# Reordering the start of a joint image and text attention block: scale-weight chunks, batch-1 transposes, shift rows

## The chip, the cores and the metric

The kernel runs on one core of a Trainium2 chip. A core has five engines with instruction streams of their own: TensorE (PE) for matmuls and transposes, VectorE (DVE), ScalarE (ACT), GpSimd (POOL), and SyncE (SP), which here issues transfers. The metric is the device time of one execution in microseconds, and the median of several runs is compared. The span is the time from the first to the last instruction of one profiled execution.

## The reference

Two batches of 256 image tokens and 32 text tokens, width D = 1152, bfloat16. Each stream is normalized, modulated, projected to Q, K and V, attended jointly, projected back, gated and added to its input.

```
mod_i = (silu(c) @ wmod_img).reshape(B, 6, 1, D)      # shift, scale, gate are the first three; text alike
hi    = layernorm(x_img) * (1 + sci) + shi            # text: ht, with its own weights
qi, ki, vi = split(hi @ wqkv_img)                     # text: qt, kt, vt
q, k, v = concat(text, image) along the tokens
p   = softmax(q @ k^T * D**-0.5)
a   = p @ v
out_i = x_img + gai * (a[image] @ wo_img)             # text alike
```

## The kernel before

The width is cut into KT = 9 column tiles of 128; the 512 image rows are four row tiles (0 and 1 are batch 0, 2 and 3 batch 1). Every weight matrix is a tile of 128 x 9 x 1152 in one of five slots, and is loaded by SP's queue in the order of the code (lines 96 to 116): x_img in two transfers, the scale part of the modulation weights (`w_sc_i`) in chunks of weight rows given by `SCC` (line 99), the V weights (`w_v_i`) in chunks of 1, 2, 3 and 3 rows, then the shift weights, Q, K and the rest whole.

The image V is not made from the modulated input. The kernel keeps two transposed inputs: `hS_i`, normalized x times (1 + scale), for V (the shift's part of V is worked out apart, in `shift_v_rows`, and added when attention is evicted), and `xT_i`, modulated in place with scale and shift, for Q and K.

The start runs as follows, in the order written out by hand. Nearly every PE instruction passes `mm` or `tr` (lines 61 and 64), which pin it in program order, as `pin` does for the DVE and ACT operations of this stage.

- `warm_up(n)` issues n matmuls of 512 columns on zeros, whose result nobody reads.
- `x_transposes(k0, b)` (line 204) does six PE transposes of three column tiles of one batch into one PSUM tile, and returns a function that issues the copy to `xT_i` (line 214). The PSUM tile is from the pool `ps_tr` (two banks) for the first two of batch 0, else from `ps_mm` (six banks).
- `sc_cols(r0, r1)` (line 198) adds the weight rows r0 to r1 to the scale sums, nine matmuls of 2 columns a row, into one `ps_mm` bank. When row 8 is in, DVE adds 1 (line 273), and `x_scale(k0, k1, b)` makes `hS_i`, one DVE operation for each column tile.
- `v_open(ids, k0, k1)` (line 227) does the V matmuls (512 columns each) of the tiles `ids` for the weight rows k0 to k1. A tile (i, cc) is row tile i and column half cc, and holds one `ps_mm` bank from its first matmul until it is evicted after row 8. `A0` is four tiles of batch 0, `A1` two of batch 1: six banks in all. Tiles (2, 1) and (3, 1) and the last 128 columns (`v_last`) follow later.
- `mod_rows_of(w_sh_i, sT32)` does the 36 matmuls of the image shift. DVE transposes the result (line 302), and DVE and ACT modulate `xT_i` (lines 314 and 317). The x_txt transfer stands behind that on ACT's queue (line 318).

A bank of a pool is taken again when the readers of its last content are done, so a matmul or a transpose into it can wait on ACT or DVE.

Of the kernel before, what the change touches and what calls it, by code (L numbers as in the profile page):

```python
# [14 lines left out]
def kernel(  # L15
# [14 lines left out]
    nc = tc.nc  # L30
# [4 lines left out]
    B, NI, D = x_img.shape  # L35
    NT = x_txt.shape[1]
    P = 128
    KT = D // P
# [19 lines left out]
    pin = tc.keep_in_program_order  # L58

    def mm(*a, **k):  # L60
        return pin(nc.tensor.matmul(*a, **k))  # L61

    def tr(*a, **k):
        return pin(nc.tensor.transpose(*a, **k))  # L64
# [17 lines left out]
    K8 = KT - 1  # L82
# [13 lines left out]
    for b in range(B):  # L96
        nc.sync.dma_start(x_i[:, b * TPB:(b + 1) * TPB, :], x_img[b].rearrange("(p t) d -> p t d", t=TPB))  # L97

    SCC = (0, 3, 5, 7, K8, KT)
    for r0, r1 in zip(SCC, SCC[1:]):  # L100
        nc.sync.dma_start(w_sc_i[:, r0:r1, :], sc_v[:, r0:r1, :])  # L101
    for r0, r1 in ((0, 1), (1, 3), (3, 6), (6, KT)):
# [23 lines left out]
    def warm_up(n):  # L126
        for _ in range(n):
            mm(wps[:], lhsT=warm[:, 0:P], rhs=warm[:], start=True, stop=True)
# [24 lines left out]
    def evac(out_ap, in_ap):  # L153
        if evac_idx[0] % 2 == 0:
            nc.vector.tensor_copy(out_ap, in_ap)  # L155
        else:
            nc.scalar.copy(out_ap, in_ap)  # L157
        evac_idx[0] += 1
# [27 lines left out]
    def ln_norm(x_ap, mean, rstd, np_, out_ap):  # L186
        pin(nc.vector.tensor_scalar(out_ap, x_ap, mean, rstd[0:np_, :], op0=ALU.subtract, op1=ALU.mult))
# [10 lines left out]
    def sc_cols(r0, r1):  # L198
        for kt in range(r0, r1):
            for j in range(KT):  # L200
                mm(sc_ps[:, j, :], lhsT=w_sc_i[:, kt, j * P:(j + 1) * P], rhs=sT[:, kt, :],
                   start=(kt == 0 and j == 0), stop=(kt == KT - 1), skip_group_check=True)

    def x_transposes(k0, b):
        tr_pool = b == 0 and k0 < 6
        tp = (ps_tr if tr_pool else ps_mm).tile([P, 3, NI], bf, tag="tr" if tr_pool else "mm", name="tp")
        for kt in range(k0, k0 + 3):
            for t in range(TPB):
                i = b * TPB + t
                tr(tp[:, kt - k0, t * P:(t + 1) * P], xn_i[:, i, kt * P:(kt + 1) * P], ident[:])  # L210
        dst = xT_i[:, k0:k0 + 3, b * NI:(b + 1) * NI]

        def copy_out():
            pin(nc.scalar.copy(dst, tp[:]) if b == 0 or k0 == 6 else nc.vector.tensor_copy(dst, tp[:]))

        return copy_out

    def x_scale(k0, k1, b):
        for kt in range(k0, k1):
            pin(nc.vector.tensor_scalar(hS_i[:, kt, b * NI:(b + 1) * NI], xT_i[:, kt, b * NI:(b + 1) * NI],  # L220
                                        sc1_i[:, kt, b:b + 1], None, op0=ALU.mult))
# [5 lines left out]
    def v_open(ids, k0, k1, kt_major=True):  # L227
        for key in ids:
            if key not in accs:
                accs[key] = ps_mm.tile([P, VW], f32, tag="mm", name="vps")  # L230
        loop = [(kt, key) for kt in range(k0, k1) for key in ids] if kt_major else \
            [(kt, key) for key in ids for kt in range(k0, k1)]
        for kt, (i, cc) in loop:
            mm(accs[(i, cc)][:], lhsT=hS_i[:, kt, i * P:(i + 1) * P], rhs=w_v_i[:, kt, cc * VW:(cc + 1) * VW],
               start=(kt == 0), stop=(kt == KT - 1), skip_group_check=True)
            if kt == KT - 1:
                evac(v_i[:, i, cc * VW:(cc + 1) * VW], accs[(i, cc)][:])

    A0 = [(0, 0), (1, 0), (0, 1), (1, 1)]
# [16 lines left out]
    r3, r2 = ln_rstd(m3[:, 1:2], P), ln_rstd(s2[:, 2:3], P, sign=-1.0)  # L256
    ln_norm(x_i[:, 3, :], m3[:, 0:1], r3, P, xn_i[:, 3, :])
    ln_norm(x_i[:, 2, :], s2[:, 0:1], r2, P, xn_i[:, 2, :])
    x_transposes(0, 0)()
    x_transposes(3, 0)()  # L260
    x_transposes(6, 0)()
    sc_cols(0, 3)
    warm_up(3)
    sc_cols(3, 5)
    warm_up(1)
    sc_cols(5, 7)
    x_transposes(0, 1)()
    out31 = x_transposes(3, 1)
    sc_cols(7, K8)
    sc_cols(K8, KT)  # L270
    out61 = x_transposes(6, 1)
    out61()
    pin(nc.vector.tensor_scalar_add(sc1_i[:], sc_ps[:], 1.0))
    x_scale(0, 3, 0)
    x_scale(0, 3, 1)
    out31()
    for b in range(B):
        x_scale(3, 6, b)
    for b in range(B):
        x_scale(6, KT, b)  # L280
    v_open(A0, 0, 3)
    v_open(A1, 0, 3)
    v_open(A0 + A1, 3, KT - 2)
    v_open(A0 + A1, KT - 2, KT, kt_major=False)
# [4 lines left out]
    def group(w, kt, g):  # L289
        return w[:, kt, :].rearrange("p (c g l) -> p g c l", g=NGG, l=LW)[:, g]  # L290

    def mod_rows_of(w, lhs):
        gps = ps_tr.tile([P, KT, LW], f32, tag="tr")
        for kt in range(KT):
            for g in range(NGG):
                mm(gps[LW * g:LW * g + LW], lhsT=lhs[:, kt, :], rhs=group(w, kt, g),
                   start=(kt == 0), stop=(kt == KT - 1), tile_position=(0, LW * g))
        return gps

    def mod_cols_of(gps, name):  # L300
        t = const.tile([P, KT, LW], f32, name=name)
        nc.vector.transpose(t[:].rearrange("p c l -> p (c l)"), gps[:].rearrange("p c l -> p (c l)"))
        return t

    p_sh = mod_rows_of(w_sh_i, sT32)
    sh_i = mod_cols_of(p_sh, "shc")
    v_open([(2, 1)], 0, 4)
    nc.vector.tensor_copy(shT32[:, :, 0:B], sh_i[:, :, 0:B])
    hT_i = xT_i
    for kt in range(KT):  # L310
# [5 lines left out]
            else:  # L316
                nc.scalar.activation(h, h, ACT.Identity, bias=sh_i[:, kt, b:b + 1], scale=sc1_i[:, kt, b:b + 1])
    pin(nc.scalar.dma_start(x_t[:], xt_flat[:, :]))
    v_open([(2, 1)], 4, KT)
    v_open([(3, 1)], 0, KT)  # L320

    def v_last():
# [301 lines left out]
```

## Time and profile before

| | |
|---|---|
| median of 13 runs | 122.09 us (121.58 to 123.31) |
| the profiled execution: its time, its span | 121.76 us, 120.0 us |
| PE busy | 114.0 us, 95% of the span |
| VectorE, ScalarE, GpSimd busy | 56.0, 34.4, 11.1 us |
| moved by DMA | 40.88 MB, 341 GB/s over the span |
| V matmuls (128x512) | 325 ns mean of one with the last ones' 128 columns, 18.0 us |

In the 40 slices each digit is the busy share of 3 us in tenths. A row of a timeline gives the start and the busy time in us, engine, line, operation, tiles and count, and in brackets how long the engine stood before it and what ended that. [...] Line 61 is the helper `mm` and line 64 the helper `tr`. A row of the chain is start, duration and what it was; a row of the waits gives the total in us, how often, and the longest. SPq and ACTq are transfers being issued on these queues, and the time to landing runs from the issue.

### The profile page before, as it was taken

Reading aid. Unit: us, or ns where it says so; the run is one execution under the profiler, and the core shown is the slowest. Engines: PE = TensorE matmul, PEld = TensorE weight load, DVE = VectorE, ACT = ScalarE, POOL = GpSimd, SP = SyncE. Lnnn points to the kernel's source line nnn. Section 1 sums busy time; section 2 is a strip of 40 time slices with the busy share of each in tenths; the row PEclk is TensorE's granted clock in tenths of the full one; section 3 lists DMA queues with packets and bytes.
Section 4 is the critical chain, followed back from the end, with each engine's and each line's share of the span. In section 5 each row is a group of like instructions: output and inputs, shape, how many; then the busy total and the mean of one; then the engine's idle time right before and its main releaser. Section 6 shows DMA issues by size and latency. Waiting matters only on the chain.

```text
span 120.0 us, 2599 instructions
## 1 busy us (share of the span) xinstructions
PE 114.0 (95%) x1112; PEld 67.3 (56%) x1121; DVE 56.0 (47%) x146; ACT 34.4 (29%) x73; POOL 11.1 (9%) x28
## 2 busy tenths in 40 slices
PE   5999889999999999999999999999999999999970
PEld 2248734445664444544448448486777766567650
DVE  1677590066837222131721203037785756666670
ACT  4899600046713104201011111125348610000000
POOL 7400000000000000000000000000222707100000
PEclk9999999999999999999999999999999999999998
DMA  4999999999999999999999999999999992420232
GB/s 134 368 376 390 401 403 413 412 413 413 404 374 413 404 411 413 413 410 414 404 413 409 418 399 414 410 408 409 415 398 409 416 367 66 148 98 0 98 81 72
DMA packets 18502, 40.88 MB, mean 341 GB/s; under 512 B 907, under 2 KB 1435, under 8 KB 18491
## 3 DMA queue, kind: packets, MB, share of 16 engines
q1 hardware_dynamic: 17616, 39.56, 84.6%
q0 software_dynamic: 480, 0.89, 2.3%
q10 hardware_dynamic: 395, 0.26, 0.7%
q8 instruction: 9, 0.15, 0.5%
q14 instruction: 2, 0.02, 0.0%
HBM read 39.38 MB, written 1.34 MB: 339 GB/s over the span
## 4 chain that ended last, share of the span: by engine, by line
PE 83%; DMA 9%; SPq 3%; DVE 1%; issue 1%
PE ps L61 51%; PE vps L61 14%; DMA t<-in_wqkv_img_dram 9%; PE gps L61 6%; PE aps L61 6%; PE sps L61 4%; SPq L101 2%; PE pT_ps L64 1%; SPq L97 1%; DVE tmp L565 1%; DVE o L566 0%; SPq L103 0%; PE tpt L64 0%
## 5 line engine op out<-in xcount | busy, mean ns | idle before, releaser
L61 PE MATMUL ps<-xT_i,t 128*128 128x512 bf16 x156 | 35.5, 379 | 0.4 <-issue 0.2
L61 PEld LDWEIGHTS <-t 128*128 128x128 bf16 x405 | 22.8, 98 | 19.4 <-issue 0.7
L61 PE MATMUL ps<-t,aT 128*128 128x384 bf16 (+3 forms) x153 | 20.2, 308 | 0.0
L61 PE MATMUL vps<-t,hS_i 128*128 128x512 bf16 (+1 forms) x106 | 18.0, 325 | 0.7 <-DVE hS_i L220 0.3
L61 PEld LDWEIGHTS <-aT 128*128 128x128 bf16 (+1 forms) x153 | 13.0, 101 | 7.1 <-issue 0.5
L61 PEld LDWEIGHTS <-hS_i 128*128 128x128 bf16 x108 | 9.0, 98 | 9.4 <-issue 0.8
L155 DVE CAST qkT<-ps 128x512 bf16<-128x512 f32 (+1 forms) x6 | 3.8, 635 | 15.4 <-PE ps L61 15.4
L61 PE MATMUL wps<-warm 128*128 128x512 bf16 x26 | 8.8, 494 | 1.3 <-DVE warm L121 1.2
L435 POOL DMA_DIRECT2D mod_scratch<-g_sb x4 | 2.5, 633 | 80.0 <-ACT g_sb L157 80.0
L565 DVE TENSOR_TENSOR tmp<-ps,gb 128x384 bf16<-128x384 f32 (+2 forms) x13 | 6.8, 526 | 6.4 <-PE ps L61 6.3
L333 DVE TENSOR_SCALAR qkT<-ps 128x512 bf16<-128x512 f32 (+1 forms) x5 | 3.3, 665 | 10.8 <-PE ps L61 10.8
L335 ACT ACTIVATE qkT<-ps 128x512 bf16<-128x512 f32 (+1 forms) x6 | 3.3, 552 | 15.5 <-PE ps L61 15.5
L157 ACT CAST qkT<-ps 128x512 bf16<-128x512 f32 (+1 forms) x5 | 2.8, 564 | 16.6 <-PE ps L61 16.6
L155 DVE CAST v_i<-vps 128x512 bf16<-128x512 f32 x5 | 3.4, 688 | 8.3 <-PE vps L61 8.3
L61 PE MATMUL aps<-pT,v_i 128*128 128x288 bf16 x36 | 6.7, 287 | 0.0
L61 PE MATMUL gps<-t,sT 128*32 128x288 bf16 x180 | 6.4, 287 | 0.0
L61 PEld LDWEIGHTS <-warm 128*128 128x128 bf16 x27 | 2.9, 117 | 5.2 <-issue 2.8
L537 DVE TENSOR_SCALAR aT<-aps,svc 128x288 bf16<-128x288 f32 x9 | 4.7, 518 | 2.4 <-PE aps L61 2.3
L61 PEld LDWEIGHTS <-sT 128*32 128x32 bf16 x180 | 4.3, 96 | 2.1 <-issue 1.5
L157 ACT CAST v_i<-vps 128x512 bf16<-128x512 f32 x4 | 2.3, 585 | 11.0 <-PE vps L61 11.0
L61 PE MATMUL sps<-qkT 128*128 128x288 bf16 (+1 forms) x54 | 5.5, 287 | 0.0
L539 ACT ACTIVATE aT<-aps,svc 128x288 bf16<-128x288 f32 x9 | 4.5, 500 | 2.5 <-PE aps L61 2.5
(94 smaller groups left out, 105.2 us busy)
## 6 DMA issues: line engine op xcount, KB each, us to landing
t<-in_wmod_txt_dram SPq DMA_DIRECT2D x3, 2592.0 KB, 18.9
t<-in_wqkv_txt_dram SPq DMA_DIRECT2D x3, 2592.0 KB, 15.7
t<-in_wmod_img_dram SPq DMA_DIRECT2D x2, 2592.0 KB, 18.6
t<-in_wqkv_img_dram SPq DMA_DIRECT2D x2, 2592.0 KB, 22.5
t<-in_wo_img_dram SPq DMA_DIRECT2D x1, 2592.0 KB, 18.0
t<-in_wo_txt_dram SPq DMA_DIRECT2D x1, 2592.0 KB
t<-in_wqkv_img_dram SPq DMA_DIRECT2D x2, 864.0 KB, 11.7
x_i<-in_x_img_dram SPq DMA_DIRECT2D x2, 576.0 KB, 4.1
```

The source lines that it names most:

```text
L61: return pin(nc.tensor.matmul(*a, **k))
L64: return pin(nc.tensor.transpose(*a, **k))
L97: nc.sync.dma_start(x_i[:, b * TPB:(b + 1) * TPB, :], x_img[b].rearrange("(p t) d -> p t d", t=TPB))
L101: nc.sync.dma_start(w_sc_i[:, r0:r1, :], sc_v[:, r0:r1, :])
L155: nc.vector.tensor_copy(out_ap, in_ap)
L157: nc.scalar.copy(out_ap, in_ap)
L333: nc.vector.tensor_scalar_mul(out_ap, in_ap, SCALE)
L335: nc.scalar.mul(out_ap, in_ap, SCALE)
L435: nc.gpsimd.dma_start(gsc[si, b, :].rearrange("(g j) -> g j", g=NGG), g_sb[b:P:32, :])
L537: nc.vector.tensor_scalar(dst, aps[:], bias, None, op0=ALU.add)
L539: nc.scalar.activation(dst, aps[:], ACT.Identity, bias=bias)
L565: nc.vector.tensor_mul(tmp[:, 0:n], ps[:, 0:n], gb[:, b, c0:c0 + n])
```

## The change

The first scale chunks are rows 0 to 3 and 4 to 6 instead of 0 to 2, 3 to 4 and 5 to 6, and three of the four warm-up matmuls between them are gone. The copies of columns 3 to 5 go to DVE and the others to ACT, in both batches. Batch 1's three groups of transposes move: the first stays behind scale row 6, the second moves behind row 8, and the third to behind the first three weight rows of `A0`; the scalings follow in a new order. The shift rows move from before V tile (2, 1) to behind it, and this tile is no longer cut in two.

```diff
-    SCC = (0, 3, 5, 7, K8, KT)
+    SCC = (0, 4, 7, K8, KT)
...
-            pin(nc.scalar.copy(dst, tp[:]) if b == 0 or k0 == 6 else nc.vector.tensor_copy(dst, tp[:]))
+            pin(nc.vector.tensor_copy(dst, tp[:]) if k0 == 3 else nc.scalar.copy(dst, tp[:]))
...
-    x_transposes(0, 0)()
-    x_transposes(3, 0)()
-    x_transposes(6, 0)()
-    sc_cols(0, 3)
-    warm_up(3)
-    sc_cols(3, 5)
+    for out in [x_transposes(k0, 0) for k0 in (0, 3, 6)]:
+        out()
+    sc_cols(0, 4)
     warm_up(1)
-    sc_cols(5, 7)
-    x_transposes(0, 1)()
-    out31 = x_transposes(3, 1)
+    sc_cols(4, 7)
+    out01 = x_transposes(0, 1)
     sc_cols(7, K8)
     sc_cols(K8, KT)
-    out61 = x_transposes(6, 1)
-    out61()
+    out31 = x_transposes(3, 1)
+    out01()
     pin(nc.vector.tensor_scalar_add(sc1_i[:], sc_ps[:], 1.0))
     x_scale(0, 3, 0)
-    x_scale(0, 3, 1)
+    v_open(A0, 0, 3)
+    out61 = x_transposes(6, 1)
     out31()
-    for b in range(B):
-        x_scale(3, 6, b)
-    for b in range(B):
-        x_scale(6, KT, b)
-    v_open(A0, 0, 3)
+    out61()
+    for k0 in (0, 3, 6):
+        for b in range(B):
+            if k0 or b:
+                x_scale(k0, k0 + 3, b)
     v_open(A1, 0, 3)
     v_open(A0 + A1, 3, KT - 2)
     v_open(A0 + A1, KT - 2, KT, kt_major=False)
...
+    v_open([(2, 1)], 0, KT)
     p_sh = mod_rows_of(w_sh_i, sT32)
     sh_i = mod_cols_of(p_sh, "shc")
-    v_open([(2, 1)], 0, 4)
...
     pin(nc.scalar.dma_start(x_t[:], xt_flat[:, :]))
-    v_open([(2, 1)], 4, KT)
     v_open([(3, 1)], 0, KT)
```

## The prediction

> **What bounds the kernel now.** I read the 40 slices first, then the chain that ended last, then the waits of PE (TensorE), then the timelines of PE, ScalarE (ACT) and VectorE (DVE) around the start of the V matmuls.
>
> ```profile
> PE   5999889999999999999999999999999999999970
> DMA  4999999999999999999999999999999992420232
> ```
>
> PE and the DMA engines are both full, so the slices don't say which sets the end. The chain (start, duration, what) does:
>
> ```profile
> 4.92 10.84 DMA t<-in_wqkv_img_dram
> 15.76 0.04 issue
> 15.80 0.38 PE vps L61
> 16.18 0.05 issue
> 16.23 10.52 PE vps L61 x48
> 26.76 1.22 PE gps L61 x36
> ```
>
> The second chunk of the V weights (rows 1 and 2) lands at 15.76. From 15.80 the chain is PE work, piece after piece, up to 115.88; only two DVE operations on the last output follow. So the end is set by when the V matmuls get their second weight chunk, plus every PE instruction and every PE wait behind that moment. The waits of PE in the first 45 us (total us, times, longest) agree:
>
> ```profile
> PE vps L61 <- DVE hS_i L220: 0.3, 1, 0.3
> PE vps L61 <- DMA t<-in_wqkv_img_dram: 0.3, 1, 0.3
> ```
>
> Ahead of 15.80 PE has slack; behind it there is none. The rows at the seam (start, busy us, idle before in brackets):
>
> ```profile
> 13.18 0.67 PE L61 MATMUL sc_ps<-sT,t 128*128 128x2 bf16 x18
> 13.71 0.49 PE L64 MATMUL tp<-ident,xn_i 128*128 128x128 bf16 x6
> 14.51 1.04 PE L61 MATMUL vps<-t,hS_i 128*128 128x512 bf16 x4 [0.31 <-DVE hS_i L220]
> 15.80 10.95 PE L61 MATMUL vps<-t,hS_i 128*128 128x512 bf16 x49 [0.26 <-DMA t<-in_wqkv_img_dram]
> ```
>
> The six transposes at 13.71 are the last of batch 1 (columns 6 to 8). PE then waits for DVE, does the four V matmuls that need weight row 0, and waits for the landing. The copy of those six:
>
> ```profile
> 14.24 0.80 ACT L214 COPY xT_i<-tp 128x768 bf16<-128x768 bf16 x1 [1.11 <-PE tp L64]
> ```
>
> This copy, too, is over before 15.80: it costs nothing today.
>
> **Part 1: first chunks and warm-ups, 0.** The first scale chunk grows from 3 rows to 4. The 3-row chunk lands at 9.13 (issued 1.63, 7.5 to landing), the next 2 rows at 10.6 (2.10 + 8.5): 0.73 us a row, so 4 rows land at about 9.87. PE is at its scale matmuls at 9.95 today; nothing is lost. The chunk up to row 6 ends with the same byte as before, at about 12.0, which is when PE waits 0.2 us for it today. Behind that come 27 small matmuls in place of 18 (18 took 0.47 from start to next start: 27 take 0.70, to 12.74), six transposes in place of twelve (0.67 for 12: 0.33, to 13.08), row 7 (0.24), and row 8, which lands at 13.44 (3.94 + 9.5). So the scale sums end at about 13.7, as today (13.71). The three dropped warm-up matmuls lie in the wait for the 12.0 landing and give nothing back.
>
> One transfer less shifts the rest of SP's queue: in the built program a transfer waits for the one eight places ahead. The fourth V chunk now waits for the second x_img transfer (landed about 5.7) instead of the first scale chunk, and is issued there instead of at 9.12. All bytes keep their order in a queue that moves 389 to 415 GB/s in every 3 us between 9 and 33 us, so landings don't move: 0. Bounds: 0.1 us later; 0.4 us earlier, since PE's four row-0 matmuls end their slots at 14.51 + 4 x 0.219 = 15.39 and it can't use the landing before.
>
> [...] The row first: eight warm-ups from 1.23 took 3.59 us (0.45 each) and V matmuls from 16.23 took 10.52/48 = 0.219 each, so a half-rate PE is plain in the spacing here (the granted clock reads 1.00 for both). Between the last early warm-up (8.73) and 14.51 PE has four wide matmuls today and will have one, with 81 two-column matmuls and short gaps of up to about 0.7 us. [...]
>
> **Part 2: order of transposes, +1.18 us.** Copies change engine (batch 0 columns 3 to 5 to DVE, 0.55; batch 1 columns 0 to 2 to ACT, 0.80): both land before the scale sums are used at 13.88, or are needed only after 15.8. Batch 1's columns 3 to 5 transposes move to the place of the old last six (13.7), ahead of V, in slack. The first V matmul still waits for DVE's first scaling (sum + 1 at 13.88, scaling from 14.17), so 14.51 stands, and the four row-0 matmuls are done before 15.76.
>
> But the last six transposes now stand behind all twelve matmuls of the first four V tiles, so behind the landing. Eight matmuls from 15.80 bring PE to T = 15.80 + 8 x 0.219 = 17.55. There:
>
> - The six transposes take PE 0.33 (half of 12 in 0.67), up to T + 0.33. Before, they filled slack; here nothing covers them.
> - Then V tile (2,0), row 0, goes at once: it takes the bank of the columns 3 to 5 transposes, copied by DVE at about 15.3.
> - Then V tile (3,0), row 0, needs a bank. The pool has six: four hold the open V tiles (0,0), (1,0), (0,1), (1,1), one has just gone to (2,0), and the sixth holds those transposes. In the built program this matmul waits on ACT, which can only be their copy. By the rows above the last transpose result is there 0.49 after the first started, ACT starts 0.04 later, and copies for 0.80: T + 1.33. About 0.07 passes from the end of an engine's write to PE's start (DVE's first scaling, 14.17 + 0.27, to PE at 14.51): T + 1.40.
>
> Without the edit (3,0) would start at T + 0.22. PE is 1.18 us late: 0.33 for transposes and 0.85 standing. Everything of V, shift rows and Q is queued behind that matmul. Bounds: 0.33, if the bank were free, to 1.5, if the copy starts 0.3 later.
>
> DVE loses nothing: its eighteen scalings end at 18.25 today; now the last three wait for that copy (18.88) and end about 19.6, while PE wants them at weight row 6, about 23.9. Weight rows 3 to 5 have landed by 18.1 and 6 to 8 by 20.2, ahead of PE today and more so then.
>
> **Part 3: shift rows one V set later, 0.** The 36 shift matmuls go behind the nine of V tile (2,1) instead of before them: the same PE work in another order. Today they start without a wait, at 26.69, on weights that landed just before (issued 10.59, and to landing):
>
> ```profile
> t<-in_wmod_img_dram SPq DMA_DIRECT2D x1, 2592.0 KB, 16.0
> ```
>
> 10.59 + 16.0 = 26.6: this execution has no wait there to remove. With the move they end at about 27.98 + 1.18 + 1.97 = 31.13 (1.97 is nine matmuls). Behind them hang DVE's transpose and twelve modulations, which end 3.9 us after the rows today (31.86 against 27.98): 35.0. Q starts at 35.19 + 1.18 = 36.4, so 1.3 us of cover stands; without it each late us would cost one. The x_txt transfer, queued on ACT behind the modulations, goes from 28.56 to about 31.7 and lands (6.4) at 38.1 in place of 35.0; its statistics on DVE, 36.08 today and else 37.3, start 0.8 later. The Q eviction queued behind them on DVE is late by under 1 us with five more banks rotating, and the text transposes, 46.95 today, have 7 us of slack. The Q weights land at 33.7 (12.01 + 21.7). SP's later weight loads that wait for PE move with PE; GpSimd's queue is not touched.
>
> **Sum.** 0 + 1.18 + 0. Span 120.0 to 121.2; the profiled time 121.76 to 122.94. The median of the runs is 0.33 above the profiled execution, so I predict **123.2** for the median (+0.9%). From no change, a measurement here can tell about 0.5%, 0.61 us.
>
> **Rivals.**
> 1. *The stall isn't there, only the transposes cost.* +0.33: 122.4. For it: a pool that hands out banks in another order. Against it: six banks, five held, and the wait on ACT in the built program. Chance 0.06.
> 2. *The shift weights are late in the usual run (not slower).* In this execution they land 0.1 us before use. Where DMA is a little slower, today's kernel stands at 26.7 and the changed one, which comes 3 us later, doesn't. The price is that wait, minus 1.18: from 0.57 us of wait on the change is within 0.5%, at 1.18 it is even (122.1), and only beyond 1.8 is it faster. For it: the 0.1 us margin, and runs up to 123.31. Against it: the median is only 0.33 above a run with no such wait, and a slow DMA delays 15.76 in both kernels. Chance 0.12.
> 3. [...] Chance 0.07.
> 4. *My mechanism*: 0.75, with 0.8 to 1.5 us, so 122.9 to 123.6.
>
> **How the numbers follow.** Below 122.4 lie most of rival 2 and half of rival 1; above 123.9 rival 3 and a little of mine: 122.4 to 123.9 leaves out about 2 in 10. Faster: the far end of rival 2 and an earlier second chunk with it, 0.04. Same: the rest of rival 2 and most of rival 1, 0.13. Slower: 0.83.
>
> **What would show it.** In the changed profile: scale sums ending at about 13.7; the V wait for the second chunk still ending near 15.8; six transposes at about 17.5; a PE wait of about 0.8 us on ACT's copy (line 214) ahead of V tile (3,0); shift rows ending near 31; the chain pure PE from there, and a span of about 121.2. The prediction is wrong if the second chunk lands far from 15.8, if PE doesn't stand at the copy, if the V matmuls are spaced over 0.3 us, or if the runs of before turn out to stand at the shift rows.

## The result and the profile after

The changed kernel takes 124.14 us in the median of 11 runs (123.56 to 125.68), the kernel before 122.21 us over the 48 runs beside it: ratio 1.017, 95% interval 1.0136 to 1.0203. It is slower by 1.9 us where I forecast 1.1, and outside the range of 122.4 to 123.9. The ratios in this document leave out the longest executions of a kernel, and below these are mostly ones in which PE's clock fell, so medians and counts by granted clock stand beside them.

The first row that differs is the granted clock over the 40 slices, before:

```profile
PEclk9999999999999999999999999999999999999998
```

And after, with the row of the DMA engines:

```profile
PEclk9999869999999999999999999999999999999999
DMA  4999999999999999999999999999999942301222
```

Slices 5 and 6 (12 to 18 us) fall. In stretches of 0.2 us the clock is 1.00 up to 14.3, 0.50 to 17.7, and 1.00 again: one fall of 3.4 us, and V starts inside it. The 3.41 us ahead of it and the fall itself (stretch, its length, PE busy, count, clock, DMA share, GB/s):

```profile
10.91:14.32 3.41, 2.21 (x68) 1.00 1.04 402
14.32:17.73 3.41, 2.92 (x9) 0.50 1.04 406
```

PE's timeline (start, busy us, idle before) at the seam:

```profile
12.27 0.83 PE L61 MATMUL sc_ps<-sT,t 128*128 128x2 bf16 x27 [1.11 <-DMA t<-in_wmod_img_dram]
12.96 0.49 PE L64 MATMUL tp<-ident,xn_i 128*128 128x128 bf16 x6
13.29 0.84 PE L61 MATMUL sc_ps<-sT,t 128*128 128x2 bf16 x18
13.99 0.53 PE L64 MATMUL tp<-ident,xn_i 128*128 128x128 bf16 x6
14.79 2.31 PE L61 MATMUL vps<-t,hS_i 128*128 128x512 bf16 x5 [0.28 <-DVE hS_i L220]
17.32 1.67 PE L61 MATMUL vps<-t,hS_i 128*128 128x512 bf16 x6 [0.22 <-issue]
18.83 0.50 PE L64 MATMUL tp<-ident,xn_i 128*128 128x128 bf16 x6
19.16 0.38 PE L61 MATMUL vps<-t,hS_i 128*128 128x512 bf16 x1
20.21 10.95 PE L61 MATMUL vps<-t,hS_i 128*128 128x512 bf16 x49 [0.67 <-ACT xT_i L214]
```

A few matmuls are missing from the traces. Here it is the one warm-up left in this stretch (only its weight load is on record, at 11.00), so that the wait of 1.11 is nearer 0.9, and one of the first twelve V matmuls, which is the 0.22 at 17.32.

The V matmuls from 14.79 are 0.43 us apart until about 17.7, against 0.219 in the kernel before (10.52/48). There one lasts 0.38 by the profile, so they overlap, and what one costs is read from the distance of the starts. At 20.21 PE has waited for ACT's copy, as forecast. The chain of the changed kernel shows the same two pieces in a row:

```profile
14.79 2.31 PE vps L61 x5
...
17.32 1.67 PE vps L61 x6
18.99 0.35 PE tp L64 x6
19.34 0.02 issue
19.36 0.81 ACT xT_i L214
20.17 0.04 issue
20.21 7.93 PE vps L61 x36
```

Further down the chain leaves PE for the softmax of DVE and ACT, which it never did before, and comes back at the first attention matmul. The wait of PE there:

```profile
PE aps L61 <- DVE pT L519: 0.3, 1, 0.3
```

The profiled executions (121.76 and 124.25 us, spans 120.0 and 122.3) can be set side by side step by step:

| | before | after | late by |
|---|---|---|---|
| first V matmul | 14.51 | 14.79 | 0.28 |
| first twelve V matmuls of `A0` end (18.83 is the start of the next transposes; 15.80 + 8 x 0.219 before) | 17.55 | 18.83 | 1.28 |
| first matmul of V tile (3,0) (17.55 + 0.22 before) | 17.77 | 20.21 | 2.44 |
| first Q matmul | 35.12 | 37.59 | 2.47 |
| first attention matmul | 88.97 | 91.76 | 2.79 |
| last PE piece of the chain ends | 115.88 | 118.67 | 2.79 |

The last scale chunk landed at 13.71 instead of 13.44, which is 0.27 of the 0.28. The twelve V matmuls took 4.04 us, where full clock makes it 12 x 0.219 = 2.63: 1.41 for the clock. Before, the same twelve took 3.04 with 0.41 of waiting for the second V chunk, and this wait is gone. Transposes and copy add 1.16, the attention 0.32. After the chain's last PE piece the changed kernel needs about 0.4 less to the end of its span, which leaves about 2.3, the difference of the spans.

In all 12 executions whose clock is recorded the mean granted clock of the changed kernel is 0.986 or 0.972: one stretch of 3.4 us at half clock in 122 us, or two. Seven executions with one took 123.87 in the median, five with two 125.23.

### The profile page after: what moved, and what is told of

It is laid out like the page before. It is cut to its first block, busy times and chain, and to the rows that moved or that the text cites. A ratio compares the mean times of both kernels' runs of the same rounds, so it can differ in the third digit from the quotient of the medians.

```text
span 122.3 us, 2591 instructions
## 1 busy us (share of the span) xinstructions
PE 113.7 (93%) x1108; PEld 67.0 (55%) x1118; DVE 56.0 (46%) x146; ACT 34.5 (28%) x73; POOL 11.1 (9%) x28
## 4 chain that ended last, share of the span: by engine, by line
PE 77%; DMA 8%; DVE 6%; ACT 2%; SPq 2%; issue 1%; DVEq 0%; ACTq 0%
PE ps L61 50%; PE vps L61 15%; DMA t<-in_wmod_img_dram 8%; PE aps L61 6%; PE gps L61 4%; ACT e L473 2%; SPq L101 1%; DVE nmx L470 1%; DVE pb L477 1%; DVE pb L479 1%; ACT xT_i L214 1%; SPq L97 1%; PE sps L61 1%; DVE rs L475 1%; DVE tmp L561 1%
## 5 line engine op out<-in xcount | busy, mean ns | idle before, releaser
L61 PE MATMUL vps<-t,hS_i 128*128 128x512 bf16 (+1 forms) x105 | 19.3, 338 | 1.3 <-ACT xT_i L214 0.7
L61 PE MATMUL wps<-warm 128*128 128x512 bf16 x23 | 6.7, 452 | 1.2 <-DVE warm L121 1.2
L61 PE MATMUL aps<-pT,v_t 128*128 128x288 bf16 x18 | 5.1, 286 | 0.0
L61 PE MATMUL ps<-hT_t,t 128*128 128x64 bf16 x162 | 5.1, 193 | 0.0
```

## The experiments

Theory A: the late transposes cost 1.18 us as forecast, and the dropped warm-ups let the clock fall. Theory B: the clock falls because of the coarser chunk or the new order. "Fell" counts executions with a mean granted clock of 0.99 or less; "clock up" is the median of the others, beside that of the kernel before in the same runs.

| kernel | median | ratio (95%) | fell | clock up, kernel before |
|---|---|---|---|---|
| changed | 124.14 | 1.017 (1.0136 to 1.0203) | 12 of 12 | none |
| changed, warm-ups back | 122.63 | 1.004 (1.001 to 1.006) | 1 of 12 | 122.63, 122.20 |
| before, without three warm-ups | 123.92 | 1.003 (0.999 to 1.007) | 10 of 12 | 122.25, 122.20 |
| before, last transposes late | 123.71 | 1.013 (1.010 to 1.016) | 3 of 7 | 123.48, 122.20 |
| changed, warm-ups back, other bank | 121.83 | 0.995 (0.992 to 0.998) | 2 of 11 | 121.39, 122.20 |
| before, chunks 4, 3, 1, 1 | 121.63 | 0.997 (0.994 to 1.000) | 2 of 12 | 121.53, 121.97 |
| before, shift rows later | 122.57 | 1.002 (0.997 to 1.006) | 5 of 12 | 121.86, 121.97 |
| before, six tiles on row 0 | 122.94 | 1.008 (1.005 to 1.011) | 6 of 7 | 122.48 (one), 121.97 |
| changed, warm-ups back, transposes early | 121.98 | 0.999 (0.996 to 1.001) | 5 of 12 | 121.80, 121.97 |
| changed, two warm-ups | 124.26 | 1.012 (1.008 to 1.016) | 5 of 6 | 122.94 (one), 121.94 |
| other bank, six warm-ups | 123.12 | 1.007 (1.003 to 1.010) | 8 of 12 | 122.12, 121.94 |
| before, chunks, shift rows, six warm-ups | 121.60 | 0.998 (0.995 to 1.001) | 3 of 12 | 121.46, 121.94 |
| changed, warm-ups back but earlier | 123.88 | 1.012 (1.008 to 1.015) | 10 of 12 | 122.84 (two), 122.03 |
| other bank, six warm-ups, again | 122.36 | 1.001 (0.997 to 1.005) | 4 of 9 | 122.07, 122.03 |

The kernel before itself fell in 16 of the 104 executions that ran beside these.

**The warm-ups put back in the changed kernel.**

```diff
     sc_cols(0, 4)
-    warm_up(1)
+    warm_up(4)
     sc_cols(4, 7)
```

> The changed kernel with the three dropped warm-up matmuls put back (four in a row behind scale row 3). Theory A (the late transposes cost 1.18 us, and the dropped warm-ups let PE's clock fall for one or two windows of 3.4 us): the granted clock is that of the kernel before (0.997), the V matmuls are 0.22 us apart from the first on, PE still stands about 0.7 us at ACT's copy, and the time is 1.2 us over the kernel before (ratio 1.010). Theory B (the clock falls because of the coarser chunk or the new order, whatever the warm-ups): granted clock stays at 0.986, ratio stays at 1.016.

The clock stays up in 11 of 12, and 1.5 us of the median are gone (124.14 - 122.63; the kernel before had the same median beside both, 122.21 and 122.24). Its timeline has the V matmuls at full pace and the same wait for ACT's copy:

```profile
11.04 0.81 PE L61 MATMUL wps<-warm 128*128 128x512 bf16 x3
12.05 0.83 PE L61 MATMUL sc_ps<-sT,t 128*128 128x2 bf16 x27 [0.20 <-DMA t<-in_wmod_img_dram]
...
14.70 2.97 PE L61 MATMUL vps<-t,hS_i 128*128 128x512 bf16 x11 [0.31 <-DVE hS_i L220]
17.51 0.50 PE L64 MATMUL tp<-ident,xn_i 128*128 128x128 bf16 x6
17.84 0.38 PE L61 MATMUL vps<-t,hS_i 128*128 128x512 bf16 x1
18.89 10.95 PE L61 MATMUL vps<-t,hS_i 128*128 128x512 bf16 x49 [0.67 <-ACT xT_i L214]
```

From the first late transpose to V tile (3,0) it is 18.89 - 17.51 = 1.38 us, and 1.40 was forecast. Theory B falls as the cause of the 12 in 12. But what is left over the kernel before is 0.4 us and not 1.2; some part of the change must win back.

**The warm-ups alone taken from the kernel before.**

```diff
     sc_cols(0, 3)
-    warm_up(3)
     sc_cols(3, 5)
```

> The kernel before without its three warm-up matmuls behind scale row 2; nothing else. Theory A: the clock falls to half for 3.4 us as the V matmuls start; at 0.43 us apart from 14.5 to 17.65 PE does about 7 of them where it did 12, so about 1.1 us is lost (ratio 1.009), and about 2.5 us where the clock falls for two windows. Theory B: no fall, ratio 1.000.

The clock fell in 10 of 12, and the median is 1.7 us up; the two others took 122.25, no more than the kernel before with its clock up. So the warm-ups' time costs nothing and their absence costs the clock. The profiled execution is one of the two, so no trace shows where the clock falls in this kernel.

**The late transposes alone.**

```diff
-    out61 = x_transposes(6, 1)
-    out61()
...
     v_open(A0, 0, 3)
+    out61 = x_transposes(6, 1)
+    out61()
```

(In this kernel the scalings of columns 6 to 8 follow the copy.)

> The kernel before with one thing moved: the last six transposes of batch 1 and their copy stand behind the first three weight rows of the first four V tiles. Theory A: granted clock as before, 0.33 us of transposes behind the landing of the second V chunk and about 0.8 us of standing at ACT's copy: 1.2 us (ratio 1.010). Rival (the stall is a follower of the slow clock, or the bank is free): 0.35 us at most (ratio 1.003).

With the clock up (four executions) 123.48 against 122.20: 1.28 us, the forecast of transposes and stall to 0.1. It fell in 3 of 7, with all warm-ups in place, which theory A doesn't say.

**The bank.** The warm-ups back, and:

```diff
-        tr_pool = b == 0 and k0 < 6
+        tr_pool = k0 < 6 if b == 0 else k0 == 6
```

> The changed kernel with the warm-ups put back and the last six transposes of batch 1 in a bank of the two-bank pool, so that V tile (3,0) needn't wait for their copy. Theory A: the clock stays up and the stall is gone; what is left is 0.33 us of transposes behind the landing (ratio 1.003). Rival (PE stands there for another reason than the bank, such as the scalings on DVE): still about 1.2 us (ratio 1.010).

PE's wait for ACT's copy is gone from the waits, and V tile (3,0) follows the transposes at once:

```profile
16.50 0.50 PE L64 MATMUL tp<-ident,xn_i 128*128 128x128 bf16 x6
16.84 11.17 PE L61 MATMUL vps<-t,hS_i 128*128 128x512 bf16 x50
```

So it was the bank. With the clock up this kernel is 1.24 us below the one with the warm-ups back only; 0.83 of it is the wait (18.89 against 17.84 + 0.22), and nothing here accounts for the rest. That it beats the kernel before here (0.995) did not hold when a close relative ran on another chip (below).

**The chunks alone.** What wins back? In the traces of the two kernels with the old chunks in this set PE stands longer than 0.26 us for the second V chunk: 1.35 us without the warm-ups, 0.89 with the late transposes (the profile names DVE, whose scalings were done over 1 us before). The wait without the warm-ups is the longest of the first row's two, the other is in the second row:

```profile
PE vps L61 <- DVE hS_i L220: 1.7, 2, 1.4
17.26 0.58 PE L61 MATMUL vps<-t,hS_i 128*128 128x512 bf16 x1 [0.89 <-DVE hS_i L220]
```

In the two with the new chunks the fifth V matmul, the first to need that chunk, starts only 0.2 us later than its slot.

```diff
-    SCC = (0, 3, 5, 7, K8, KT)
+    SCC = (0, 4, 7, K8, KT)
...
-    sc_cols(0, 3)
-    warm_up(3)
-    sc_cols(3, 5)
-    warm_up(1)
-    sc_cols(5, 7)
+    sc_cols(0, 4)
+    warm_up(4)
+    sc_cols(4, 7)
```

> The kernel before with the first scale chunks as in the changed kernel (4, 3, 1, 1 rows) and all four warm-up matmuls behind the first. The changed kernel with its warm-ups back came out cheaper than its stall of 0.85 us and 0.33 us of transposes, because V weight rows 1 and 2 were there when PE wanted them. Theory C (one transfer less lets the second V chunk land earlier): PE doesn't wait for it after the four row-0 matmuls, ratio 0.994. Theory F (where the 16 KB fetch of instructions on one DMA engine falls sets when that chunk lands: at the start of V in the kernel before, about 1 us later where twelve PE instructions fewer stand ahead of V): the count of PE instructions ahead of V is unchanged here, the fetch still falls at the start of V, PE still waits 0.3 us or more for the chunk, ratio 1.000.

0.44 us faster with the clock up, ratio 0.997, its interval just under 1. The 54 V matmuls of the first six tiles run on with hardly a wait (the row doesn't break at the fifth, which is 0.1 us late):

```profile
14.96 11.93 PE L61 MATMUL vps<-t,hS_i 128*128 128x512 bf16 x54 [0.31 <-DVE hS_i L220]
```

Theory C got over half of its gain. Theory F falls as I wrote it: the fetch came between 15.75 and 16.0, about 1 us behind the start of V, with as many PE instructions ahead as before. Over all traces the two still go together. In the five with the old chunks the fetch starts 0.9 to 2.7 us before the second V chunk lands (at 15.7 to 17.2). In those with the new chunks and the clock up it starts no more than 0.2 us before the first matmul on that chunk, which comes 0.1 to 0.3 us late. No run separates the fetch from the number of transfers.

**The shift rows alone.**

```diff
+    v_open([(2, 1)], 0, KT)
     p_sh = mod_rows_of(w_sh_i, sT32)
     sh_i = mod_cols_of(p_sh, "shc")
-    v_open([(2, 1)], 0, 4)
...
-    v_open([(2, 1)], 4, KT)
     v_open([(3, 1)], 0, KT)
```

> The kernel before with the shift rows behind V tile (2,1), nothing else. My step: no wait stands at the shift rows, so 0 (ratio 1.000). Rival 2 of the prediction (the shift weights are late in usual runs): 0.3 us or more faster (ratio 0.997 or less).

Ratio 1.002 (0.997 to 1.006), with the clock up 0.11 us less: no change that can be told. In this trace, with the old chunks, the fifth V matmul starts at 15.77, 0.29 us late, against 0.41 in the kernel before and 1.5 without the warm-ups, so the wait changes from execution to execution. The clock fell in 5 of 12, against 4 of 30 of the kernel before beside it, although this edit lies 12 us behind the start of V. Where it fell isn't on record, but counts of this size say little about an edit; 12 of 12 against 1 of 12 does.

**Six tiles on row 0**, to cover that wait (with the shift rows as above):

```diff
-    v_open(A0, 0, 3)
-    v_open(A1, 0, 3)
-    v_open(A0 + A1, 3, KT - 2)
+    v_open(A0 + A1, 0, KT - 2)
```

(The copies of batch 1's columns 0 to 2 and 3 to 5 go to ACT and DVE, the second ahead of the scalings.)

> The kernel before with six V tiles instead of four on weight row 0, so that PE has 0.44 us more of work before it needs the second V chunk; the copy of batch 1's columns 3 to 5 comes earlier to free the bank, and the shift rows stand behind V tile (2,1). If PE's wait for that chunk is what starts the PE-only chain, the wait shrinks by up to 0.44 us: ratio 0.9965. If the chain starts elsewhere (DVE's scalings): 1.000.

It fell in 6 of 7, and the one other took 122.48. The expectation missed. In its trace, which fell, PE does the first 63 V matmuls without a wait for that chunk, but the first ones at half clock, so whether the wait is covered at full clock can't be read from it.

**The transposes early again**, in the changed kernel with its warm-ups:

```diff
     out31 = x_transposes(3, 1)
     out01()
+    out61 = x_transposes(6, 1)
...
-    v_open(A0, 0, 3)
-    out61 = x_transposes(6, 1)
     out31()
     out61()
+    v_open(A0, 0, 3)
```

> The changed kernel with the warm-ups back and the last six transposes ahead of V again: its chunks and its place of the shift rows, without stall and without transposes behind the landing. Theory C: 1.18 us less than the changed kernel with warm-ups back alone (ratio 1.004), so ratio 0.994. Theory F: the fetch falls at the start of V again, the wait for the second V chunk is back, ratio 1.000.

0.17 us under the kernel before with the clock up, between the two theories. Chunks and shift rows alone make -0.44 - 0.11 = -0.55. The rest is the wait at attention: every trace of the changed kernel and of those built from it shows 0.3 to 0.4 us there, and none of those built from the kernel before does. In the changed kernel the third of the five softmax exponentials on ACT starts only when DVE has scaled the second tile's weights, a wait that the kernel before doesn't have:

```profile
  DVE nmx L470: 2.5, 3
  DVE pb L479: 1.3, 1
```

(What ACT waited for around the tile `e` in the changed kernel: total us, times.) -0.55 + 0.33 = -0.22 agrees with -0.17. In its own trace, where V starts at 13.60, the first V matmuls on the second and third V chunk are also late, by 0.3 and 0.4. The source there is the same in both; why an edit at 10 to 35 us makes the built program wait differently at 86 us I haven't tried.

**How many warm-ups.**

```diff
-    warm_up(1)
+    warm_up(2)
```

> The changed kernel with two warm-up matmuls behind scale row 3, where it has one, the kernel before four. In the traces so far the clock fell where the 3.4 us ahead of the fall held no or one matmul of 512 columns (the changed kernel, the late transposes alone, six tiles on row 0) and stayed where they held three or more (warm-ups put back, the early transposes). If that count decides, two lie at the edge: between a tenth and nine tenths of the executions fall, and the median lies between 122.6 and 124.1. If it is only the gap in PE's work (about 0.9 us here, 1.1 with one), nearly all fall as with one, and the median is 124.0.

It fell in 5 of 6; the median of the six is 124.26. And this trace breaks my count: its clock falls at 15.57, and the 3.4 us ahead hold three V matmuls.

```profile
12.15:15.57 3.42, 2.76 (x60) 1.00 1.04 404
15.57:18.98 3.41, 3.41 (x9) 0.50 1.04 405
```

**Two more, ahead of V.** As the other bank, and:

```diff
+    warm_up(2)
     v_open(A0, 0, 3)
```

> The changed kernel with its warm-ups back, the last six transposes in the two-bank pool, and two more warm-up matmuls where PE waits for DVE's first scaling ahead of V. They fill 0.3 us of standing and should cost 0.0 to 0.1 us; if matmuls in the window decide, the clock falls in fewer executions than without them (2 of 11), and the ratio is 0.992 to 0.994, the best so far. If the filled wait delays V, 0.997.

A clear miss: fell in 8 of 12, 123.12. **The parts that gained, together**: the kernel before with the chunks, the shift rows and these two warm-ups.

> The kernel before with the changed chunks (all four warm-ups behind the first), the changed place of the shift rows, and two more warm-ups in the wait ahead of V; the transposes stay where they were. By the parts alone (chunks -0.4 us, shift rows -0.1 with the clock up) about 121.5, ratio 0.995, with the clock falling in one execution of ten or fewer. If the parts don't add (as with the changed kernel with early transposes, 0.999), 0.998.

121.60 and 0.48 us less with the clock up, as by the parts; it fell in 3 of 12. The chunks alone do as well with less.

**As many warm-ups, in another place.**

```diff
+    warm_up(3)
     sc_cols(0, 4)
     warm_up(1)
```

> The changed kernel with the three warm-up matmuls back, but ahead of the scale matmuls instead of behind row 3: as many as where the clock stayed up in 11 of 12 executions, in another place (about 9.7 to 10.4 us instead of 11.0 to 11.9), with one behind row 3 as in the changed kernel. They lie in PE's waits and cost nothing by themselves. Theory P (what counts is how long PE then has only two-column matmuls and transposes before V: 3.6 us and more here against 2.8): the clock falls in most executions, median 123.5 to 124.5. Theory N (the number of warm-ups counts): it falls in one of ten, median 122.6.

It fell in 10 of 12, 123.88: place, not number. The granted clock and the warm-ups by 3.4 us stretch of this trace (the first fence is all of PE, the second the warm-ups):

```profile
9.88:13.29 3.41, 2.61 (x74) 1.00 1.03 397
13.29:16.70 3.41, 3.41 (x35) 0.50 1.04 409
```

```profile
9.88:13.29 3.41, 0.81 (x3) 1.00 1.03 397
```

PE is busy for 2.61 of the 3.41 us ahead of the fall by the profile's measure, and all four warm-ups lie in them: three in the row, and the fourth, whose matmul is missing from the trace and whose weight load is at 11.43.

**The kernel with six warm-ups again**, for a trace of a fallen execution.

> The kernel with the bank and six warm-ups once more, for a trace of an execution whose clock falls (8 of 12 did, against 2 of 11 without the last two warm-ups). Theory P: the fall comes at the end of a 3.4 us stretch between the fourth warm-up and the start of V, as in the changed kernel. If it comes behind the start of V, the wide matmuls themselves don't keep the clock up.

It fell in 4 of 9, but not in the profiled execution, so where it falls in this kernel stays open. With the clock up it takes 122.07 against 122.03; by the parts it should be +0.11, the -0.22 above and 0.33 for the late transposes.

## Why the prediction was wrong

- **The step that failed**: the first 0 of the sum, as far as it stands for the dropped warm-ups. No run shows that term; the runs showed 1.5 in its place (124.14 - 122.63). PE's waits in the changed kernel are about 1.1 us at the longest behind its first instruction, and the clock fell in every execution. The sign of it was in my own text: the four warm-ups were the only wide matmuls between 8.7 and 14.5. In the trace of the changed kernel the 68 two-column matmuls and transposes, which the profile calls busy for 2.21 of the 3.41 us ahead of the fall, didn't keep the clock up.
- **Rival 3**, a fall of the clock, got 0.07, and should have had most of the chance. One fall costs 1.1 to 1.2 us where seven or more executions show it (124.00 - 122.84, 123.11 - 122.03, 123.17 - 122.12), two cost 2.1 where seven do (124.31 - 122.25). In the profiled execution V started 0.47 us into the fall, and the slow V matmuls also covered 0.41 of waiting.
- **Part 2**, late transposes and stall: right. 1.18 forecast; 1.28 alone with the clock up; T + 1.40 forecast for V tile (3,0), 1.38 measured in each of the four traces of the changed kernel and its relatives that have the wait. Rival 1 (no stall) is out: with another bank the wait is gone.
- **Part 1**, the chunks' landing, "0 ... 0.4 us earlier" as the bound: the chunks alone measured -0.44. The value was wrong and the bound about right. I had taken the 15.76 of one trace for a fixed time; with the old chunks it lies anywhere from 15.7 to 17.2. Why the new chunks help isn't settled: fewer transfers, or where the fetch of instructions falls.
- **Part 3**, shift rows: 0 forecast, no difference measured. Nothing speaks for rival 2: no trace with the shift rows in the old place has a wait there. The x_txt statistics started at 39.30, and nothing on PE waited for them.
- **Not seen at all**: 0.3 us at the attention.
- **The sum**: 122.09 + 1.18 makes 123.3 and not 123.2, which changes nothing here.

Without the clock the parts make +1.28 - 0.44 - 0.11 + 0.33 = +1.06, from runs on two chips. The changed kernel with its warm-ups back and the clock up measured +0.43 on one chip, its relatives with earlier or with two warm-ups +0.8 and +1.0 (three executions in all) on another. On the first the old chunks' wait was longest in the traces, which may be why; this was only argued. So the forecast of 1.1 for the time without the clock is not confirmed as a sum: the stall was there, other parts won some of it back, and how much is open. The clock is the rest, 1.5.

## What to carry to other kernels

Before dropping or moving dummy matmuls, list the wide matmuls alone over time, since small matmuls and transposes count as busy in the profile and still didn't hold the clock here (2.21 of 3.41 us ahead of the fall). No count of them was safe (below), so try the edit with several executions and read each one's granted clock. Where a pool of accumulators is full, a tile that is copied late in the same pool makes the last accumulator wait for the copy (0.67 us on ACT here): count the banks, and take another pool. A landing time from one trace is a sample: treat it as a range (that of the second V chunk was 15.7 to 17.2 here).

## What the hardware showed that I had not expected

- A clock fall isn't a matter of standing still. It came with PE 65 to 83% busy by the profile in the 3.41 us ahead (2.21 to 2.85 us in five traces), and lasted 3.41 us in four of these traces and twice that in the one with the late transposes alone.
- In these five traces the falls keep a step. The early warm-ups are 0.43 us apart up to a moment, with which the record of the granted clock begins, and 0.22 from there on; it is 4.08, 4.25, 4.72, 5.33 and 6.46 us. The fall begins 10.24 us later in the first four and 6.83 in the fifth: three and two times 3.41. Over all fifteen traces the moment lies anywhere from 3.96 to 7.12. No run here fixes it, so whether it has to do with one kernel falling in some executions and not in others is not shown.
- What brings a fall stays open. Place mattered (1 of 12 against 10 of 12 with four warm-ups each, on two chips), and two more just ahead of V went with more falls (8 of 12 and 4 of 9, against 2 of 11 without them). The number of wide matmuls in the 3.41 us ahead doesn't decide: in the trace with earlier warm-ups four stand in 9.88 to 13.29, and the clock fell to 0.50 behind them; in the one without the three warm-ups 11.02 to 14.43 has two V matmuls and PE busy for 2.54, and the clock stayed up.
- The profile counts the fetch of instructions among the transfers, in packets of 16 KB (9 in the kernel before, 0.15 MB). In the quarter microsecond from 14.25 of the kernel before the transfers show "q8 instruction", one packet; whether it delays the V chunk in flight was argued only.
- The kernel before falls too, in 16 of 104 executions, and one fall costs it about 1.1 us (123.11 - 122.03 where seven show it): a good part of its spread from 121.6 to 124.6 there.
